# The second expert choice of a two-layer mixture counts per expert on the partitions, and the constants of the choices are copied by ScalarE

## The chip, the cores and the metric

One core of a Trainium2 chip runs the whole program. The metric is the device time of one execution in microseconds (us); the engines are PE (TensorE matmul, with PEld for its weight loads), DVE (VectorE), ACT (ScalarE), POOL (GpSimd) and SP (SyncE, which issues DMAs).

## The reference, cut to what matters

Attention runs over 4 x 768 tokens of 8 heads, then a first mixture of experts, then a second one. The change lies in the second mixture. Each expert of it takes at most 384 of the 3072 tokens, and the (token, expert) pairs are served in the order of their logits:

```
cap = N // E                      # 384 tokens per expert, 8 experts
order = np.argsort(-logits.flatten())
for idx in order:
    tok, e = idx // E, idx % E
    if assigned[tok] >= 0 or counts[e] >= cap: continue
    assigned[tok] = e; counts[e] += 1
for e in range(E):
    mask = assigned == e
    out[mask] = np.maximum(x[mask] @ w1[e], 0.0) @ w2[e]
```

## The kernel before, in words

The attention and the first mixture fill the first 324 us of the profile and are not touched. The second mixture is `phase_d`, with the choosing in the class `Route2`.

**The choosing.** The greedy order is followed in eight phases. A phase finds the expert that fills up first, which tokens it gets, and takes both out of the logits `Lm` (128 partitions x 8 experts x 24 columns of tokens). To find where the first expert fills up, a phase searches a threshold on each token's best logit `v`: `NSTEP` = 5 steps, each with 32 candidate thresholds `thr` (L788). `g` (L793) marks for each of 24 token columns which thresholds each token reaches; `oh` (L783) marks each token's best expert. Matmuls of `g` with `oh` over the 128 partitions count, for each threshold, how many tokens each expert would get.

- Phase 0 counts with 24 matmuls a step (L802) that put thresholds on the partitions and experts on the columns, marks the thresholds with a full expert (L812), and one more matmul with ones (L825) counts those and spreads the number to all partitions. L826 turns it into the new lower bound `lo`.
- Phase 1, as `wide(1)` is 2, takes two token columns at once: 12 matmuls a step (L806), a subtraction (L809), a maximum over the experts (L815), a comparison (L823), and then the same matmul with ones (L825) and L826. PE is thus visited twice in a step, DVE works between the two visits, and both visits stand in PE's in-order queue.
- Phases 2 to 6 take four columns at once and count the full thresholds on DVE, with a 32x32 transpose (L820) and a reduction (L821) in place of the matmul with ones.

After the steps come `hi`, the marks of the tokens above the bounds (L831, L833), sums over them (L836, L842), the chosen expert `ei` (L849), and each token's place (L855 to L864). `ei` starts the load of that expert's weights from SP; `list` (L875) turns the places into row numbers, by which POOL gathers the token rows `xg` (L939).

**The experts.** An expert is `L1` (32 quarters: eight 128-column pieces of the hidden layer, four quarters each, a quarter being the three matmuls L961, L962, L963 of 384 columns) and `L2` (24 thirds of three matmuls of 512 columns, L975 to L977). Weights are split in high and low parts by ACT (`wh`, L923) and POOL (`wl`, L932). After each fourth quarter ACT writes `dhh` (L966) and DVE `dhl` (L968).

**The order of the work.** One loop at the end of `phase_d` writes the program, with a clock of its own, `now`. A quarter adds 0.5 to it. The choosing is a generator: each `yield lat,dur` gives the DVE time `lat` until its next piece of PE work may follow, and the PE time `dur` of that piece. `step` adds `lat` to the DVE clock and sets the piece due 0.1 after that while expert 0 runs; once `now` has reached the due time, the loop writes the piece into the program and adds `dur` to `now`. Each `dhl` adds 0.5 to the DVE clock. So these two numbers set how many quarters stand between two pieces of the choosing. All engines then run their queues in order.

Phase 1 is written while expert 0 runs, and its tail and `list(1)` come in expert 0's `L2`. The four constants `c8`, `jr`, `colid` and `p0` are copied into the PSUM tile `st_ps` by DVE at the start of phase 0 (L752, L754), behind the exit of the loop of L709, which ran no round here.

Of the kernel before, what the change touches and what calls it, by code (L numbers as in the profile page):

```python
# [6 lines left out]
F32=mybir.dt.float32; BF=mybir.dt.bfloat16; F32R=mybir.dt.float32r; I32=mybir.dt.int32; U32=mybir.dt.uint32  # L7
# [38 lines left out]
def phase_a(nc,tc,ctx,I,st):  # L46
    V=nc.vector; A=nc.scalar; T=nc.tensor; G=nc.gpsimd
    cl=ExitStack(); ld=cl.enter_context(tc.tile_pool(name="a_ld",bufs=2,side="right"))
# [7 lines left out]

    wm=K2[1][:,0].rearrange("p a b->p (a b)")[:,0:256]; V.memset(wm,1.0); wm=wm.bitcast(BF)
    def spin(k,wm=wm):
        p=ps.tile([128,4,128],F32,name="s_ps").rearrange("p a b->p (a b)")
        for _ in range(k): T.matmul(p,wm[:,0:128] if len(wm.shape)==2 else wm[:,0,0:128],wm,start=True,stop=True)  # L60
    spin(WARM)
    for i in range(2):
        t=cp.tile([128,2,12,128],F32,name=f"Q2_{i}"); Q2.append(t)
        for h in range(2):
            (G if i else V).memset(t[0:64,h,:,64:128],0.0); G.memset(t[64:128,h,:,0:64],0.0)
    for i in range(3):
# [7 lines left out]
    def load(u):  # L74
# [3 lines left out]
        def ld_k(h0,h1): nc.sync.dma_start(kt[:,h0:h1],I['k'][b,:,2*g+h0:2*g+h1,:])  # L78
# [10 lines left out]
        if u==0: nc.sync.dma_start(cst,I['cst'])  # L89
        if u==2: yield; prep_v(1,V)  # L90
        ld_k(1,2); ld_q(1,2)
# [7 lines left out]
    def prep_k(u,h):  # L99
        d=U[u]; kt,ks=d['kt'],d['ks']  # L100
        V.tensor_reduce(ks[:,h],kt[:,h,39:39+S].rearrange("p (n k)->p n k",k=32),AX.X,OP.max)
    def prep_k2(u,h,cpy):
# [10 lines left out]
    def prep_v(u,eng):  # L113
        d=U[u]; vn,vv=d['vn'],d['vv']
        vs2=wk.tile([96,64],F32,name="vs2",bufs=2); w=1024
        if eng is V: V.tensor_reduce(vs2,vn[:,w:2*w].rearrange("p (k d)->p d k",d=64),AX.X,OP.add); w//=2
        while w>=64:
            G.tensor_tensor(vn[:,0:w],vn[:,0:w],vn[:,w:2*w],op=OP.add); w//=2  # L118
        if eng is V: G.tensor_tensor(vn[:,0:64],vn[:,0:64],vs2,op=OP.add)
        G.tensor_scalar(vs2,vn[:,0:64],1.0/32,None,op0=OP.mult)  # L120
        for h in range(4):
            nc.sync.dma_start(vv[0:24,:,h,0:64],vs2[24*h:24*h+24,None,:].to_broadcast([24,12,64]))
# [612 lines left out]
class Route2:  # L735
    def __init__(self,nc,tc,cp,wk,ps,I,st):
        self.nc,self.tc,self.cp,self.wk,self.ps,self.st=nc,tc,cp,wk,ps,st
        cc=st['cc']
        self.jr=cc[:,0:32]; self.wsc=cc[:,32:37]; self.p0=cc[:,37:38]
        self.Lm=st['Lm']; self.asg=st['asg']; self.r=st['rrow']  # L740
        self.pos={}
        st['io']=cp.tile([128,8,3],I32,name="io"); self.th=cp.tile([128,2],F32,name="th")
        self.ws=cp.tile([128,5],F32,name="ws"); self.nM=cp.tile([128,1],F32,name="nM")

        q=ps.tile([128,512],F32,name="st_ps",bufs=1); o=0; self.q={}
        for nm,w in (('v',24),('jr',32),('c8',8),('mx',24),('gl',48),('tm',24),('sat',8),('s8',8),('dm',48),('fo',8),('kp',24),('x0',24),('an',24),('pos',24),('si',24),('bi',24),('sf',24),('bf',24),('colid',24),('p0',1),('oc',12)):
            self.q[nm]=q[:,o:o+w]; o+=w
    def state(self,nm,dt=None):
        return self.q[nm].bitcast(dt) if dt else self.q[nm]
    def init_state(self):  # L750
        V=self.nc.vector; st=self.st
        for nm,src in (('c8',st['c8']),('jr',self.jr)): V.tensor_copy(self.q[nm],src)  # L752
        yield
        for nm,src in (('colid',st['colid']),('p0',self.p0)): V.tensor_copy(self.q[nm],src)  # L754
        yield
    def wide(self,ph): return 2 if ph<3 else 4
    def psum(self):
        return self.ps.tile([128,512],F32,name="rt_ps",bufs=1)
# [9 lines left out]
    def phase(self,ph):  # L768

        nc,st,wk=self.nc,self.st,self.wk; V=nc.vector; T=nc.tensor  # L770
        B3=[128,8,24]; B4=[128,2,8,24]; Lm=self.Lm; c8=st['c8']
        ini=self.init() if ph==0 else iter(()); inq=self.init_state() if ph==0 else iter(()); Q=self.state
        next(inq,None)
        v=Q('v'); V.tensor_reduce(v,Lm.rearrange("p e c->p c e"),AX.X,OP.max)
        if ph: yield 0.4,0
        cand=wk.tile(B3,BF,name="p_cand"); V.tensor_tensor(cand,Lm,v[:,None,:].to_broadcast(B3),op=OP.is_ge)
# [4 lines left out]
        mx=Q('mx'); V.tensor_reduce(mx,cand.rearrange("p e c->p c e"),AX.X,OP.max)  # L781
        next(ini,None)
        oh=wk.tile(B3,BF,name="p_oh"); V.tensor_tensor(oh,cand,mx[:,None,:].to_broadcast(B3),op=OP.is_equal)  # L783
        th=self.th; lo=th[:,0:1]; hi=th[:,1:2]; ws=self.ws
        if ph<7:
            low=self.nM
            for s in range(NSTEP):
                thr=wk.tile([128,32],F32,name="p_thr"); V.tensor_scalar(thr,Q('jr'),ws[:,s:s+1],low,op0=OP.mult,op1=OP.add)  # L788
                if s==0: yield 1.3,0
                g=wk.tile([128,24,32],BF,name="p_g")  # L790
                for c0,c1 in (((0,12),(12,20),(20,24)) if ph==0 else ((0,24),)):
                    B=[128,c1-c0,32]
                    V.tensor_tensor(g[:,c0:c1],v[:,c0:c1,None].to_broadcast(B),thr[:,None,:].to_broadcast(B),op=OP.is_ge)  # L793
                if s==0: next(inq,None)
                nw=self.wide(ph) if ph>=1 else 1
                yield ((2.3+0.2*nw if ph>=2 else 1.4) if s else 1.1),(0.7 if ph<1 else 0.8/self.wide(ph))
                p=self.psum()

                anys=wk.tile([J,1],BF,name="p_any")
                if ph<1:  # L800
                    if ph==0: T.matmul(p[0:J,0:8],st['mone'][:,0:J],st['capr'],start=True,stop=False)
                    for c in range(24): T.matmul(p[0:J+(ph>0),0:8],g[:,c,0:J+(ph>0)],oh[:,:,c],start=(ph>0 and c==0),stop=(c==23))  # L802
                else:

                    n=self.wide(ph)
                    for c in range(0,24,n): T.matmul(p[0:32*n,0:8*n],g[:,c:c+n,:].rearrange("p c j->p (c j)"),oh[:,:,c:c+n].rearrange("p e c->p c e"),start=(c==0),stop=(c==24-n))  # L806
                    d=wk.tile([128,8],F32,name="p_d"); x=self.r
                    for q in range(n-1,0,-1):
                        V.tensor_tensor(d[32*q-32:32*q],x[32*q:32*q+32],p[32*q:32*q+32,8*q:8*q+8],op=OP.subtract); x=d  # L809
                if ph==0:  # L810
                    sat=wk.tile([J,8],BF,name="p_sat")
                    V.tensor_scalar(sat,p[0:J,0:8],0.0,0.0,op0=OP.is_ge,op1=OP.max,accum_out=anys)  # L812
                else:
                    R=32; sat=wk.tile([32,8],F32,name="p_sat1"); e=wk.tile([32,1],F32,name="p_e")
                    V.tensor_tensor_reduce(out=sat,in0=p[0:R,0:8],in1=self.r[0:R] if ph<1 else d[0:R],scale=1.0,scalar=-1e9,op0=OP.subtract,op1=OP.max,accum_out=e)  # L815
                if ph>=2:

                    an=wk.tile([128,1],F32,name="p_an4")
                    for q in range(4): V.tensor_scalar(an[32*q:32*q+R],e,0.0,None,op0=OP.is_ge)
                    tr=wk.tile([128,32],F32,name="p_tr"); V.transpose(tr,an.to_broadcast([128,32]))  # L820
                    p=wk.tile([128,1],F32,name="p_cnt"); V.tensor_reduce(p,tr[:,0:J],AX.X,OP.add)  # L821
                else:
                    if ph: V.tensor_scalar(anys,e[0:J],0.0,None,op0=OP.is_ge)  # L823
                    yield (0.7 if ph else 0.35),0.05
                    p=self.psum(); T.matmul(p[:,0:1],st['ones_b'][0:J,:],anys,start=True,stop=True)  # L825
                V.tensor_scalar(lo,p[:,0:1],ws[:,s:s+1],low,op0=OP.mult,op1=OP.add); low=lo  # L826
            V.tensor_scalar(hi,lo,ws[:,NSTEP-1:NSTEP],None,op0=OP.add)
        else:
            for x in (lo,hi): V.tensor_copy(x,self.nM)
        gl=Q('gl').rearrange("p (s c)->p s c",s=2); gs=wk.tile([128,2,24],F32,name="p_gl")  # L830
        for x in (gl,gs): V.tensor_tensor(x,v[:,None,:].to_broadcast([128,2,24]),th[:,:,None].to_broadcast([128,2,24]),op=OP.is_ge)  # L831
        og=wk.tile(B4,BF,name="p_og"); rs=wk.tile([128,2,8],BF,name="p_rs")
        V.tensor_tensor(og,oh[:,None,:,:].to_broadcast(B4),gl[:,:,None,:].to_broadcast(B4),op=OP.mult)  # L833
        if ph: yield (3.0 if 2<=ph<7 else 1.0),0
        with nc.allow_low_precision("counts up to 24 are exact"):
            V.tensor_reduce(rs,og,AX.X,OP.add)  # L836

# [4 lines left out]
        p=self.psum(); T.matmul(p[:,0:16],st['ones_b'],rs.rearrange("p s e->p (s e)"),start=True,stop=True)  # L842
# [3 lines left out]
        dm=Q('dm').rearrange("p (s c)->p s c",s=2); t2=wk.tile([128,2],BF,name="p_t2")  # L846
# [4 lines left out]
        fo=Q('fo'); V.tensor_scalar(fo,s8,m8,None,op0=OP.is_equal)  # L851
# [7 lines left out]
        kp=Q('kp'); V.scalar_tensor_tensor(kp,x[:,1],float(CAP),dm[:,1],op0=OP.is_le,op1=OP.mult)  # L859
        x0=Q('x0'); V.tensor_mul(x0,x[:,0],dm[:,0])  # L860
        V.tensor_mul(x[:,1],x[:,1],kp)
        pos=Q('pos',I32)
# [265 lines left out]
```

## Time and profile before

| | |
|---|---|
| median of 3 runs | 687.71 us (686.41 to 689.97) |
| the profiled execution, its own time | 682.42 us |
| its span, first to last instruction | 680.8 us |
| granted TensorE clock, mean over the span | 0.946 |
| PE, DVE, ACT, POOL busy | 604.4, 508.0, 314.2, 359.0 us |

The time of an execution is the span and 1.6 us around it. A group of instructions in a row of the profile is named by its line, engine and operation, then out<-in by the program's tile names. Matmuls overlap: one of 384 columns lasts 0.34 us in the rows and the next starts 0.17 us after it.

### The profile page before, as it was taken

What the parts mean: (1) busy time and instruction counts of PE and PEld (TensorE: products, weight loads), DVE (VectorE), ACT (ScalarE), POOL (GpSimd) and SP (SyncE); (2) the same over time, 40 slices, a digit from 0 to 9 for tenths busy, and PEclk for the clock granted to TensorE, in tenths of its full rate; (3) what the DMA queues carried; (4) which work ended last, traced back from release to release, by engine and by line L of the source; (5) the groups of instructions that cost most, each with busy time, mean ns of one, the idle gap of its engine ahead of it and who ended that gap; (6) DMA issues with size and microseconds to landing.
All of it is one profiled execution on the core that took longest, in us unless ns stands there. A gap on an engine that the chain in (4) does not pass through costs nothing.

```text
span 680.8 us, 12765 instructions
## 1 busy us (share of the span) xinstructions
PE 604.4 (89%) x4424; PEld 494.0 (73%) x4427; DVE 508.0 (75%) x1896; ACT 314.2 (46%) x672; POOL 359.0 (53%) x388
## 2 busy tenths in 40 slices
PE   8769896899788999989447999999999999999996
PEld 5658775778466776666226778888797978879895
DVE  5788985999896899994675778788888888862120
ACT  6557774787235676461014235162533426154521
POOL 5234323535462463761016359494876939399841
PEclk9889997999689999898559999999999999999999
DMA  9999999969309968610026063453626254385201
GB/s 258 256 241 249 241 234 206 281 115 339 136 16 324 294 207 287 204 62 23 2 87 208 2 227 115 166 175 124 202 76 203 79 187 155 139 258 180 105 1 46
DMA packets 59778, 114.22 MB, mean 168 GB/s; under 512 B 13537, under 2 KB 23521, under 8 KB 58944
## 3 DMA queue, kind: packets, MB, share of 16 engines
q1 hardware_dynamic: 49968, 79.37, 40.6%
q0 software_dynamic: 9744, 34.02, 15.1%
q8 instruction: 35, 0.57, 0.4%
q14 instruction: 31, 0.25, 0.1%
HBM read 96.54 MB, written 14.88 MB: 164 GB/s over the span
## 4 chain that ended last, share of the span: by engine, by line
PE 18%; issue 11%; POOL 11%; DVE 6%; DMA 3%; ACT 1%; POOLq 1%; DVEq 0%
POOL wl L932 9%; PE dh_ps L961 3%; PE dh_ps L962 3%; PE dh_ps L963 3%; DMA xg<-xrows,p_ix 2%; PE dz_ps L975 2%; PE dz_ps L976 2%; PE dz_ps L977 2%; POOL out_dram L982 2%; DMA wraw<-in_w1b_dram 1%; DVE p_g L793 1%; PE rt_ps L806 1%; PE dx_ps L895 1%; PE dh_ps L950 1%; ACT wh L923 1%
## 5 line engine op out<-in xcount | busy, mean ns | idle before, releaser
L932 POOL TENSOR_TENSOR wl<-wraw,wh 128x512 fp32r<-128x512 f32 x124 | 155.4, 1297 | 5.9 <-ACT wh L923 5.5
L961 PE MATMUL dh_ps<-dxh,wh 128*128 128x384 f32 x256 | 89.2, 349 | 0.7 <-ACT dxh L953 0.7
L923 ACT CAST wh<-wraw 128x512 fp32r<-128x512 f32 x128 | 73.7, 620 | 33.8 <-DMA wraw<-in_w1b_dram 33.4
L962 PE MATMUL dh_ps<-dxl,wh 128*128 128x384 f32 x256 | 86.3, 337 | 0.5 <-DVE dxl L953 0.5
L963 PE MATMUL dh_ps<-dxh,wl 128*128 128x384 f32 x256 | 86.1, 336 | 0.0
L118 POOL TENSOR_TENSOR wraw<-wraw 96x512 f32<-96x512 f32 (+4 forms) x39 | 39.9, 1023 | 80.2 <-DMA wraw<-in_v_dram 77.8
L975 PE MATMUL dz_ps<-wh,dhh 128*128 128x512 f32 x192 | 79.0, 411 | 0.0
L977 PE MATMUL dz_ps<-wh,dhl 128*128 128x512 f32 x192 | 76.0, 396 | 0.0
L976 PE MATMUL dz_ps<-wl,dhh 128*128 128x512 f32 x192 | 75.9, 395 | 0.0
L968 DVE SCALAR_TENSOR_TENSOR dhl<-dh_ps,dhh 128x384 fp32r<-128x384 f32 x64 | 35.1, 554 | 49.0 <-ACT dhh L966 48.7
L982 POOL DMA_INDIRECT out_dram<-dz,io x24 | 24.5, 1023 | 79.5 <-ACT dz L980 76.8
L966 ACT ACTIVATE dhh<-dh_ps 128x384 fp32r<-128x384 f32 x64 | 31.5, 492 | 75.7 <-PE dh_ps L963 74.8
L505 POOL TENSOR_TENSOR wl<-wraw,wh 128x512 fp32r<-128x512 f32 (+1 forms) x26 | 47.8, 1861 | 26.2 <-ACT wh L504 22.7
L980 ACT COPY dz<-dz_ps 128x512 f32<-128x512 f32 x24 | 14.1, 587 | 102.8 <-PE dz_ps L977 56.8
L138 ACT ACTIVATE p_e<-s_sb,nm 128x118 f32<-128x118 f32 x192 | 59.7, 385 | 1.1 <-DVE nm L132 1.1
L128 PE MATMUL s_ps<-kt,Q 128*128 128x118 f32 x192 | 41.4, 299 | 11.6 <-DVE kt L108 9.1
L939 POOL DMA_INDIRECT xg<-xrows,p_ix x24 | 23.3, 972 | 50.9 <-DVE rrow L871 31.3
L961 PEld LDWEIGHTS dh_ps<-dxh,wh 128*128 128x128 f32 x256 | 48.4, 189 | 1.5 <-ACT dxh L953 0.9
L962 PEld LDWEIGHTS dh_ps<-dxl,wh 128*128 128x128 f32 x256 | 48.2, 188 | 1.3 <-DVE dxl L953 1.1
L963 PEld LDWEIGHTS dh_ps<-dxh,wl 128*128 128x128 f32 x256 | 48.1, 188 | 0.0
L504 ACT CAST wh<-wraw 128x1024 fp32r<-128x1024 f32 (+1 forms) x48 | 44.2, 983 | 7.3 <-DMA wraw<-in_w1a_dram 7.1
L132 DVE CUSTOM_DVE_ANT_0 s_sb<-s_ps,cst 128x118 f32<-128x118 f32 x192 | 42.0, 275 | 5.3 <-PE s_ps L128 3.5
(359 smaller groups left out, 1466.5 us busy)
## 6 DMA issues: line engine op xcount, KB each, us to landing
wraw<-in_w1b_dram SPq DMA_DIRECT2D x15, 1024.0 KB
wraw<-in_w2b_dram POOLq DMA_DIRECT2D x14, 1024.0 KB, 7.5
wraw<-in_w2a_dram SPq DMA_DIRECT2D x12, 1024.0 KB
wraw<-in_w1a_dram SPq DMA_DIRECT2D x10, 1024.0 KB
VV<-in_v_dram SPq DMA_DIRECT2D x16, 585.0 KB
kt<-in_k_dram SPq DMA_DIRECT2D x16, 412.0 KB
qd<-in_q_dram SPq DMA_DIRECT2D x16, 384.0 KB
wraw<-in_v_dram SPq DMA_DIRECT2D x8, 768.0 KB
```

What stands on the lines that cost most here:

```text
L132: V.tensor_tensor_reduce(out=sb[:,j,:],in0=p[:,j,0:118],in1=mk,scale=-0.125,scalar=3e38,op0=OP.add,op1=OP.min,accum_out=nm[:,j:j+1])
L138: A.activation(pe[:,j,:],sb[:,j,:],AF.Exp,bias=nm[:,j:j+1],scale=-1.0)
L504: (hi.tensor_copy if hi else nc.scalar.copy)(h[:,c],t[:,c])
L505: (lo or nc.vector).tensor_tensor(l[:,c],t[:,c],h[:,c].bitcast(F32),op=OP.subtract)
L923: A.copy(h[:,c],t[:,c])
L932: eng.tensor_tensor(l[:,c],t[:,c],h[:,c].bitcast(F32),op=OP.subtract)
L961: T.matmul(q,wh[:,c],s['xh'][:,d,:],start=(d==0),stop=False)
L962: T.matmul(q,wh[:,c],s['xl'][:,d,:],start=False,stop=False)
L963: T.matmul(q,wl[:,c],s['xh'][:,d,:],start=False,stop=(d==3))
L975: T.matmul(q,s['hh'][:,f,c0],wh[:,c],start=(f==0),stop=False)
L976: T.matmul(q,s['hh'][:,f,c0],wl[:,c],start=False,stop=False)
L977: T.matmul(q,s['hl'][:,f,c0],wh[:,c],start=False,stop=(f==7))
```

## The change

In phase 1 the experts stand on the partitions in place of the thresholds. `oh` is copied four times by ACT into `oh4`, 24 columns of 4 x 8 weights. Each step has 96 matmuls: for each of the 24 token columns, four with 32 weight columns and 32 moving columns, each of the four writing its own 32 partitions of `p`, so that every partition holds the counts of expert (partition mod 8) for 32 thresholds. `rc`, made once, holds that expert's remaining room on the same partition. One DVE operation compares and counts (`cn`), a transpose and a maximum over 32 spread the largest count, and `lo` follows. L809, L815, L823 and the matmul with ones L825 are gone from phase 1, and each step visits PE once. The planner's numbers for phase 1 change: 1.9 and 1.1 for a step (1.4 and 0.4, then 0.7 and 0.05 before) and 1.6 before the sums (1.0 before).

The four constants go to PSUM by four ACT copies at the start of phase 0, in place of two DVE copies there and two after `g` of phase 0's first step.

```
+... ('p0',1),('oc',12),('sat1',32)):
     def init_state(self):
-        V=self.nc.vector; st=self.st
-        for nm,src in (('c8',st['c8']),('jr',self.jr)): V.tensor_copy(self.q[nm],src)
-        yield
-        for nm,src in (('colid',st['colid']),('p0',self.p0)): V.tensor_copy(self.q[nm],src)
-        yield
+        A=self.nc.scalar; st=self.st
+        for nm,src in (('c8',st['c8']),('jr',self.jr),('colid',st['colid']),('p0',self.p0)): A.copy(self.q[nm],src)
...
+        if ph==1:
+            rc=wk.tile([128,32],F32,name="p_rc"); V.transpose(rc,self.r[:,None,:].to_broadcast([128,4,8])); rc=rc[:,0:1]
+            oh4=wk.tile([128,24,4,8],BF,name="p_oh4")
+            for q in range(4): nc.scalar.copy(oh4[:,:,q],oh.rearrange("p e c->p c e"))
...
-                yield ((2.3+0.2*nw if ph>=2 else 1.4) if s else 1.1),(0.7 if ph<1 else 0.8/self.wide(ph))
+                yield ((2.3+0.2*nw if ph>=2 else 1.9 if ph else 1.4) if s else 1.1),(0.7 if ph<1 else 1.1 if ph<2 else 0.8/self.wide(ph))
                 p=self.psum()
+                if ph==1:
+                    for c in range(24):
+                        for q in range(4): T.matmul(p[32*q:32*q+32,0:32],oh4[:,c].rearrange("p r e -> p (r e)"),g[:,c,:],start=(c==0),stop=(c==23))
+                    cn=wk.tile([128,1],F32,name="p_cn"); sx=Q('sat1')
+                    V.tensor_scalar(sx[:,0:J],p[:,0:J],rc,0.0,op0=OP.is_ge,op1=OP.add,accum_out=cn)
+                    tr=wk.tile([128,32],F32,name="p_tr"); V.transpose(tr,cn.to_broadcast([128,32]))
+                    p=wk.tile([128,1],F32,name="p_cnt"); V.tensor_reduce(p,tr,AX.X,OP.max)
+                    V.tensor_scalar(lo,p,ws[:,s:s+1],low,op0=OP.mult,op1=OP.add); low=lo
+                    continue
...
-        if ph: yield (3.0 if 2<=ph<7 else 1.0),0
+        if ph: yield (3.0 if 2<=ph<7 else 1.6),0
```

## Rows read from the trace of the kernel before

**Rows 1.** Windows: length, each engine's busy us (instructions), granted clock, DMA share, GB/s.
```profile
368.75:408.89 40.14, 39.53 (x263) 32.05 (x263) 29.96 (x111) 12.56 (x24) 21.01 (x22) 1.00 0.31 103
...
410.90:660.00 249.10, 247.29 (x1398) 215.73 (x1399) 176.73 (x682) 102.21 (x197) 183.37 (x182) 1.00 0.43 145
```

**Rows 2.** Timeline of PE in phase 1: start, us, instructions [idle before, releaser].
```profile
364.90 0.57 PE L806 MATMUL rt_ps<-p_oh,p_g 128*64 128x16 bf16 x12
...
368.75 0.17 PE L825 MATMUL rt_ps<-p_any,ones_b 31*128 31x1 bf16 x1 [2.05 <-DVE p_any L823]
...
370.18 0.34 PE L962 MATMUL dh_ps<-dxl,wh 128*128 128x384 f32 x1
370.35 0.34 PE L963 MATMUL dh_ps<-dxh,wl 128*128 128x384 f32 x1
370.64 0.57 PE L806 MATMUL rt_ps<-p_oh,p_g 128*64 128x16 bf16 x12
371.13 0.44 PE L961 MATMUL dh_ps<-dxh,wh 128*128 128x384 f32 x1
...
386.43 0.39 PE L975 MATMUL dz_ps<-wh,dhh 128*128 128x512 f32 x1
```

**Rows 3.** Timeline of ACT and DVE before the first step's second visit to PE.
```profile
364.98 2.18 ACT L923 CAST wh<-wraw 128x512 fp32r<-128x512 f32 x4 [3.49 <-DMA wraw<-in_w1b_dram]
...
367.58 0.56 DVE L968 SCALAR_TENSOR_TENSOR dhl<-dh_ps,dhh 128x384 fp32r<-128x384 f32 x1 [4.50 <-ACT dhh L966]
368.17 0.15 DVE L809 TENSOR_TENSOR p_d<-rrow,rt_ps 32x8 f32<-32x8 f32 x1
```

**Rows 4.** Single lines (min/median/max ns, first and last start) and the DVE timeline of phase 2.
```profile
L847 DVE TENSOR_SCALAR_CACHE_REDUCE st_ps<-asg,p_m x16: 245/245/248, 345.0 to 597.4; 128x24 f32<-128x24 bf16 x16
L847 DVE DVE_READ_ACCUMULATOR st_ps<-asg,p_m x16: 142/143/146, 345.1 to 597.6; 128x1 bf16 x16
...
402.62 0.21 DVE L820 STREAM_TRANSPOSE p_tr<-p_an 128x32 f32<-128x32 f32 x1
...
403.74 0.96 DVE L793 TENSOR_TENSOR p_g<-st_ps,p_thr 128x768 bf16<-128x768 f32 x1
```

**Rows 5.** Timelines of PE and one line of ACT: small operations.
```profile
310.39 0.43 PE L611 MATMUL yt_ps<-yT,wg 128*32 128x128 f32 x8
330.35 0.82 PE L802 MATMUL rt_ps<-p_oh,p_g 128*31 128x8 bf16 x24 [1.49 <-DVE p_g L793]
405.41 0.66 PE L950 MATMUL dh_ps<-cb,xg 128*128 128x128 f32 x4
...
L193 ACT ACTIVATE g_d<-g_d 128x48 f32<-128x48 f32 x3 | 0.7, 243 | 11.5 <-DVE g_d L192 11.5
```

**Rows 6.** The start of phase 0: the loop's exit on PE and ACT, then DVE's timeline.
```profile
L709 PEldq COMPARE_BRANCH  x2: 187/248/310, 325.6 to 327.3; - x2
...
L709 ACTq COMPARE_BRANCH  x1: 38/38/38, 325.6 to 325.6; - x1
...
326.18 0.17 DVE L752 COPY st_ps<-cb 128x8 f32<-128x8 f32 x1
...
326.61 0.62 DVE L774 TENSOR_REDUCE st_ps<-Lm 128x24 f32<-128x192 f32 x1
...
328.36 0.29 DVE L763 TENSOR_REDUCE i_a<-rt_ps 128x1 f32<-128x128 f32 x1 [0.34 <-PE rt_ps L762]
...
331.20 0.15 DVE L812 TENSOR_SCALAR_CACHE_REDUCE p_sat<-rt_ps 31x8 bf16<-31x8 f32 x1
```

**Rows 7.** Timeline of PE at the border from expert 0 to expert 1.
```profile
409.52 0.56 PE L806 MATMUL rt_ps<-p_oh,p_g 128*64 128x16 bf16 x12 [0.46 <-DVE p_g L793]
...
410.72 0.44 PE L962 MATMUL dh_ps<-dxl,wh 128*128 128x384 f32 x1 [0.26 <-DVE dxl L953]
```

**Rows 8.** Windows around an idle PE in the first mixture, columns as in rows 1.
```profile
191.12:193.77 2.65, 0.01 (x2) 0.01 (x1) 2.65 (x16) 0.60 (x1) 0.63 (x2) 1.00 0.01 3
193.79:197.20 3.41, 3.41 (x35) 3.20 (x36) 2.01 (x10) 1.37 (x3) 0.96 (x1) 0.50 0.09 19
```

More of the change, by code (lines that the diff above doesn't have):

```diff
@@ L745, in __init__ @@
         q=ps.tile([128,512],F32,name="st_ps",bufs=1); o=0; self.q={}
-        for nm,w in (('v',24),('jr',32),('c8',8),('mx',24),('gl',48),('tm',24),('sat',8),('s8',8),('dm',48),('fo',8),('kp',24),('x0',24),('an',24),('pos',24),('si',24),('bi',24),('sf',24),('bf',24),('colid',24),('p0',1),('oc',12)):
+        for nm,w in (('v',24),('jr',32),('c8',8),('mx',24),('gl',48),('tm',24),('sat',8),('s8',8),('dm',48),('fo',8),('kp',24),('x0',24),('an',24),('pos',24),('si',24),('bi',24),('sf',24),('bf',24),('colid',24),('p0',1),('oc',12),('sat1',32)):
             self.q[nm]=q[:,o:o+w]; o+=w
@@ L771, in phase @@
         B3=[128,8,24]; B4=[128,2,8,24]; Lm=self.Lm; c8=st['c8']
-        ini=self.init() if ph==0 else iter(()); inq=self.init_state() if ph==0 else iter(()); Q=self.state
-        next(inq,None)
+        ini=self.init() if ph==0 else iter(()); Q=self.state
+        if ph==0: self.init_state()
         v=Q('v'); V.tensor_reduce(v,Lm.rearrange("p e c->p c e"),AX.X,OP.max)
@@ L793, in phase @@
                     V.tensor_tensor(g[:,c0:c1],v[:,c0:c1,None].to_broadcast(B),thr[:,None,:].to_broadcast(B),op=OP.is_ge)
-                if s==0: next(inq,None)
                 nw=self.wide(ph) if ph>=1 else 1
-                yield ((2.3+0.2*nw if ph>=2 else 1.4) if s else 1.1),(0.7 if ph<1 else 0.8/self.wide(ph))
+                yield ((2.3+0.2*nw if ph>=2 else 1.9 if ph else 1.4) if s else 1.1),(0.7 if ph<1 else 1.1 if ph<2 else 0.8/self.wide(ph))
                 p=self.psum()
+                if ph==1:
[7 more added lines that the diff above has]
+                    continue
                 anys=wk.tile([J,1],BF,name="p_any")
```

## The prediction

> **What bounds the kernel now.** I read the windows by stage first. From 368.75 us, in the middle of expert 0's first layer, PE is busy for 39.53 of 40.14 us, and from 410.90 to 660 for 247.29 of 249.10, at full granted clock [rows 1]. So what counts is how much PE time the second choice takes out of expert 0: every wait that it makes on PE goes to the end of the kernel one for one, and work taken off DVE or ACT counts only where PE waits for it.
>
> The timeline of PE in phase 1 comes next. A quarter of the first layer is three matmuls whose starts lie 0.17 apart, 0.52 us. A step's first visit (L806) takes PE from 370.35 + 0.17 = 370.52 to 371.13, 0.61 us; its second (L825) some 0.2, its own 0.17 and the step to the next. In the first step PE also stands still for 2.05 us before L825 [rows 2]. The timelines of DVE and ACT say why: the landing of weights let ACT start four casts at 364.98, the first `dhh` stood behind them, DVE did `dhl` at 367.58 and only then, in its order, L809 at 368.17 [rows 3].
>
> **The change, step by step: PE's visits.** Gone are five visits L825, 5 x 0.2, and the first one's wait. Each L806 becomes 96 matmuls. The trace has none of 32 by 32 in this form. The nearest are eight with 32 weight columns and 128 moving ones, each writing one quarter of the partitions: 0.43 us for all eight, while four of 128 moving columns on the whole array take 0.66 [rows 5]. That is 0.054 each against 0.165, with the run of the last one counted in both, so the quarters of the array do work side by side. A pair of load and matmul that has no other beside it takes (0.57 - 0.17)/11 = 0.036 in L806 and (0.82 - 0.17)/23 = 0.028 in L802 [rows 2, 5]. I take 24 fours of 0.03, 0.72, and the two ends of a visit, 0.61 - 11 x 0.036 = 0.21: 0.93 us a step. Bounds: 0.88, and 2.9 to 3.7 if all 96 pairs stand one after another. The work on PE grows from 5 x 0.81 = 4.05 to 4.65.
>
> Here a rule speaks against the change. The eight matmuls of L611 overlap though all of them use all 128 rows [rows 5]. The Trainium skill, page "TensorE: Matmul & The Clock Gate", section "Part 3: Packing small matmuls — row/col tiling", says that a weight load overlaps matmuls in flight only when the row group differs; by it the 96 pairs would follow one another, the upper bound, where the row gives 0.93. The row does not bear the rule out, so I go by the row; what the other would mean is a rival below.
>
> **DVE between two visits.** After the counts a step needs the comparison with its sum (like L847, 0.25, and 0.14 to read the sum), then transpose, maximum, `lo`, `thr` and `g`, which in phase 2 run from 402.62 to 404.70 [rows 4]: 0.39 + 2.08 = 2.47 us. In the first step the comparison stands where L809 stood, behind the same `dhl`, at 368.17, and `g` is done at 370.64. That is just when the second L806 starts in the kernel before [rows 2]. So the wait of 2.05 us is not gone: it moves to the next visit.
>
> How much PE does meanwhile is set by the planner. After a visit `now` has grown by 1.1, and the next is due 1.9 + 0.1 later: four quarters of 0.5 (a `dhl`'s 0.5 falls inside these and doesn't count). The visits will stand after quarters 5, 9, 13, 17 and 21. Before, by the same arithmetic with 0.4, 0.7, 0.05 and 1.4, they stood after 5, 10, 16, 21 and 26.
>
> So: first visit at 364.90; PE has it and four quarters behind it at 364.90 + 0.81 + 2.06 = 367.8, and waits until 370.65, 2.85 us, some 2.7 of them idle, as the last matmul still runs. From there a visit repeats after 0.70 + 0.17 (the last count's end) + 0.04 + 2.47 + 0.05 = 3.44 us, while PE has 0.93 + 2.06 = 3.0 of work: it waits some 0.45 in each of three. The fifth visit is at 370.65 + 3 x 3.44 = 381.0. With 0.81 and the 11 quarters left (5.7) the first layer ends at 387.5, and the visit L842 (0.2), which then stands inside it, makes that 387.7. Before, it ends at 386.43 with L842 still ahead, 386.6 [rows 2]. **The choice costs +1.0.** Bounds: -0.5, if five quarters stand between visits and nothing waits, and +2.1, if `dhl` waits for ACT's casts and adds 0.3 to each cycle.
>
> `oh4` and `rc`: four ACT copies, each near the 0.24 of L193 [rows 5], and 0.21 of DVE like L820 [rows 4]. Both engines then wait for the gathered rows of expert 0, so 0; without that cover they cost 1 us.
>
> **The start.** Two DVE copies before L774 go, 326.61 - 326.18 = 0.43 us. But DVE already waits 0.34 for PE's L762 before it starts L763 at 328.36, and PE is held by its own exit from the loop until 327.5 at the earliest (327.3 + 0.19) [rows 6]. DVE would only wait longer: 0, not -0.43. The other two copies end as the first counts do (L802 ends at 330.35 + 0.82 = 331.17, L812 starts at 331.20): 0 [rows 5, 6]. ACT leaves the loop at 325.6 and needs some 4 x 0.24. If all accesses to `st_ps` are kept in order, L774 starts at about 326.7 in place of 326.61, and the 0.34 hides that too. Bounds: -0.4, if L762 follows DVE after all, and +0.5, if the copies end only at 327.5.
>
> **The border.** The planner's clock gives phase 1 more PE time than before, 5 x (1.1 - 0.4 - 0.05) = 3.25, so its tail, the load and the gather for expert 1 are written five thirds of the second layer (0.65 each) earlier. PE is busy there; this buys only the waits at the border, 0.46 and 0.26 [rows 7]. I take -0.5, since `dxl` comes sooner; bounds 0 and -0.7.
>
> Sum: +1.0 + 0 - 0.5 = +0.5 on the profiled execution's 682.42 (its span of 680.8 and 1.6 around it): 682.9. The median of the runs shown, 687.71, lies 5.3 above that execution; I carry the difference over: **688.2 us**.
>
> **The rivals.**
> - *The clock falls.* PE's new idle time is longer than the old. After 2.65 us without work in the first mixture the clock stood at 0.50 for 3.41 us [rows 8]; after the 2.05 before L825 it did not fall [rows 1, 2]. 3.41 us at half speed lose 1.7, of which a wait of 0.45 hides part: +1.3, 689.5.
> - *The wait really goes (the other side).* If enough quarters stand between the first and the second visit, or the first `dhh` is not behind the casts, PE loses neither the 2.05 nor its successor: -2.05 + 0.6 for the visits, -0.7 at the border: -2.1, 685.6. For it speaks that the visit which waited is gone; against it the planner's four quarters, and the landing at 364.98 that the change doesn't move. It decides from 2.85 / 0.52 = 5.5 more quarters.
> - *The 96 matmuls run one after another.* A visit of 2.9 to 3.7 makes a cycle of 5.4 to 6.1, in which four quarters hardly wait. The fifth visit comes at 386.9 to 389.0, and expert 0 ends 9 to 12 later: 696 to 699. For it speaks only that L611's moving part is four times as long and its burst short. This is what the Trainium skill's rule named above would do here.
> - *The ACT copies are late*, behind ACT's exit from the loop: +0.5, 688.7.
>
> **How the numbers follow.** Forecast 0.50, the clock falls 0.22, the wait goes 0.13, one after another 0.08, late copies 0.07. A measurement of this kernel can tell about 0.5% (3.4 us) from no change. The forecast's own bounds reach from -1.6 to +2.6, 686.1 to 690.3. The range takes in the case in which the wait goes and the one in which the clock falls with its bounds (+1.3 and some +2), and the spread of the runs (1.3 below and 2.3 above their median), and leaves out the case of matmuls one after another: 684.9 to 692.0. Below 684.3 lies the lower half of the case in which the wait goes, and 0.03 of the others: 0.10. Above 691.1 lie the 96 in a row, 0.08, and a third of the clock's case: 0.15. The rest, 0.75, can't be told from no change.
>
> **What would show it.** On PE: a step's 96 matmuls in 0.9 us, a wait of 2 to 3 us before the second step's, visits after quarters 5, 9, 13, 17 and 21, and from the first quarter of expert 0 to its second layer 0.8 to 1.5 us more than before. At the start: L763 as far behind the loop's exit as before. I am wrong if the second visit finds `g` ready, if a step's matmuls last over 1.5 us, if the clock drops near 371, or if the waits at the border grow.

## The result and the profile after

The changed kernel takes 695.46 us (median of 5 runs, 693.21 to 698.48) beside 687.95 (686.41 to 689.97) of the kernel before: a ratio of 1.0113, with a 95% interval of 1.0074 to 1.0151. The change is slower by some 7.5 us. The prediction, 688.2 with a range of 684.9 to 692.0, is wrong: its likeliest case was no change that can be told, and its range ends below the result.

| | before, as shown | after |
|---|---|---|
| the profiled execution, its own time | 682.42 us | 697.96 us |
| its span | 680.8 us | 696.3 us |
| granted TensorE clock, mean over the span | 0.946 | 0.931 |
| PE, DVE, ACT, POOL busy | 604.4, 508.0, 314.2, 359.0 us | 613.1, 506.3, 317.5, 361.4 us |

The two profiled executions lie 15.5 us apart, twice what the runs say. Part of that is the spread of single executions ahead of the change: `Lm`, the last addition to the logits with which the second mixture's choosing starts, is reached at 325.8 us before and at 332.6 after, in code that nobody touched, and between 324.9 and 332.6 in the thirteen profiles of this study, the old code among the late ones too (329.9 in experiment 6). The lower mean clock is no mark of the change either: the old code of experiment 6 was granted 0.931 too. So all that follows is counted from `Lm` on, in stages, for every profile. The windows of the kernel after, from `Lm` to expert 0, then expert 0, 1, 2 and 3, 4, 5 and 6, 7, and last from expert 1's first matmul to PE's last one:

```profile
core 0: us, PE busy (x) PEld busy (x) DVE busy (x) ACT busy (x) POOL busy (x), PEclk, DMA share, GB/s
332.55:370.07 37.52, 15.16 (x185) 10.19 (x185) 27.49 (x102) 6.11 (x15) 5.55 (x7) 0.59 0.28 87
370.07:419.83 49.76, 47.63 (x723) 40.42 (x724) 36.85 (x131) 16.15 (x31) 27.97 (x27) 0.95 0.43 145
419.83:460.12 40.29, 39.88 (x250) 34.75 (x249) 32.30 (x127) 16.28 (x31) 28.34 (x29) 1.00 0.45 148
460.12:541.67 81.55, 77.62 (x439) 66.25 (x438) 65.70 (x263) 31.93 (x61) 54.84 (x57) 1.00 0.41 136
541.67:581.09 39.42, 38.65 (x221) 33.26 (x219) 32.30 (x127) 15.11 (x29) 27.70 (x29) 1.00 0.44 144
581.09:657.24 76.15, 74.05 (x391) 64.45 (x390) 40.30 (x151) 32.50 (x62) 59.93 (x60) 1.00 0.49 162
657.24:690.83 33.59, 33.59 (x169) 29.98 (x167) 4.46 (x8) 9.22 (x18) 14.81 (x17) 1.00 0.06 24
419.83:690.83 271.00, 263.79 (x1465) 228.69 (x1463) 175.06 (x673) 105.05 (x201) 185.63 (x187) 1.00 0.40 132
```

The same windows of the kernel before, in the profile of its second copy (experiment 1), for experts 2 and 3, 5 and 6, and the whole from expert 1 on; last, the whole in the profile shown first:

```profile
453.44:531.32 77.88, 77.17 (x440) 66.39 (x439) 66.67 (x267) 31.20 (x60) 55.37 (x56) 1.00 0.45 148
...
570.32:644.64 74.32, 73.67 (x391) 64.08 (x390) 40.05 (x150) 32.43 (x62) 58.17 (x58) 1.00 0.48 164
...
411.20:678.25 267.05, 264.79 (x1467) 229.85 (x1464) 177.67 (x685) 103.76 (x200) 186.31 (x187) 0.99 0.41 138
```
```profile
410.02:675.43 265.41, 263.34 (x1467) 228.17 (x1464) 177.55 (x685) 104.27 (x201) 186.38 (x187) 1.00 0.41 139
```

Before, PE was busy for nearly all of the time from expert 1 on [rows 1]. After, it is idle for 271.00 - 263.79 = 7.21 us there, where the kernel before has 265.41 - 263.34 = 2.07 in the profile shown and 2.26 in its second one. The loss lies in experts 2 and 3 and in 5 and 6, where the diff changes no instruction. What the change did to expert 0 comes near the forecast: 49.76 us from its first matmul to that of expert 1, 48.48 and 48.89 before.

The timeline of PE, the new visits of phase 1 (start, us, instructions, idle before and releaser):

```profile
375.47 0.93 PE L803 MATMUL rt_ps<-p_g,p_oh 128*32 128x32 bf16 x96
378.98 0.93 PE L803 MATMUL rt_ps<-p_g,p_oh 128*32 128x32 bf16 x96 [0.30 <-DVE p_g L795]
382.49 0.93 PE L803 MATMUL rt_ps<-p_g,p_oh 128*32 128x32 bf16 x96 [0.26 <-DVE p_g L795]
```

The 96 matmuls of a step take the 0.93 us that were forecast, a visit repeats after 3.51 (forecast 3.44), and PE waits some 0.3 at each of four visits, which with the end of the last matmul comes near the 0.45 of the forecast.

### The profile page after: what moved, and what is told of

Read it like the earlier page. It is cut to its first block, busy times and chain, and to the rows that moved or that the text cites. A ratio compares the mean times of both kernels' runs of the same rounds, so it can differ in the third digit from the quotient of the medians.

```text
span 696.3 us, 13616 instructions
## 1 busy us (share of the span) xinstructions
PE 613.1 (88%) x4842; PEld 503.7 (72%) x4842; DVE 506.3 (73%) x1893; ACT 317.5 (46%) x680; POOL 361.4 (52%) x390
## 4 chain that ended last, share of the span: by engine, by line
PE 16%; POOL 12%; issue 12%; DVE 6%; DMA 3%; ACT 1%; POOLq 1%; DVEq 0%; ACTq 0%
POOL wl L944 10%; DMA xg<-xrows,p_ix 3%; PE dz_ps L987 2%; PE dz_ps L988 2%; PE dz_ps L989 2%; PE dh_ps L973 2%; PE dh_ps L974 2%; PE dh_ps L975 2%; POOL out_dram L994 2%; DVE p_g L795 1%; PE dh_ps L962 1%; PE rt_ps L803 1%; PE rt_ps L818 1%; ACT wh L935 1%; PE rt_ps L814 1%
## 5 line engine op out<-in xcount | busy, mean ns | idle before, releaser
L128 PE MATMUL s_ps<-kt,Q 128*128 128x118 f32 x192 | 43.2, 310 | 4.9 <-DVE kt L108 4.1
```

What stands on the lines that cost most here:

```text
L128: T.matmul(p[:,j,0:118],d['q2'][:,h,w,:],d['k2'][:,h,w//2,:] if w%2 else d['kt'][:,h,64*w:64*w+118],start=True,stop=True)
```

## The experiments

All kernels are compared with the kernel before on their own chip; a run's ratio has its 95% interval behind it. Line numbers are those of each kernel: before, `list`'s second form is L898, the counts from phase 2 on L806, the transposes of gathered rows L950; in the changed kernel they are L910, L818 and L962. Phase 2 takes two columns at once like phase 1 (12 matmuls a visit); four at once begin with phase 3 (6 matmuls). "From expert 1 on" is always from its first matmul to PE's last one; the 265.4 and 271.0 of the expectations, which say "to the last instruction", are read so too. The code cuts are shortened.

The first four ran together. **1. The kernel before, once more**, without an edit.

> The kernel before, unchanged, for a second profile: which stages move by themselves. Every theory expects a ratio of 1.000. If the 6.8 us by which the profile after reached the second mixture later (332.6 against 325.8) is spread of runs, this profile moves there by several us too, and by less than 1 us from the first quarter of expert 1 to the end (265.4).

Measured: 1.0034 (0.9994 to 1.0073). So a ratio within some 0.4% of 1 says nothing here. Both expectations of the profile failed: it reaches `Lm` only 0.2 us later (experiment 6 shows the spread there), and from expert 1 on it takes 267.05 us, 1.6 more than the first. Expert 1 holds that (42.24 beside 40.67): TensorE's clock is granted at 0.50 there for 3.41 us from 412.90 on, and half of these, some 1.7 us, are lost against 1.00 by estimate.

**2. The changed kernel with later due times.**

```
-   yield ((2.3+0.2*nw if ph>=2 else 1.9 if ph else 1.4) if s else 1.1), ...
+   yield ((2.3+0.2*nw if ph>=2 else 2.4 if ph else 1.4) if s else 1.1), ...
...
-   if ph: yield (3.0 if 2<=ph<7 else 1.6),0
+   if ph: yield (3.0 if 2<=ph<7 else 2.1),0
```

> The changed kernel with its due times later, 2.4 in place of 1.9 a step and 2.1 in place of 1.6 before the sums: five quarters between two visits, so that the choosing of experts 2 to 7 stands in PE's order where it stood before (tail of phase 1 after quarter 33, list of expert 1 after the 46th piece). Theory of the order (the loss is that the choosing moved against the experts by five pieces): expert 0 costs 0 to 2 us more than before, from expert 1 to the end 265 to 267 us as before, ratio 1.000 to 1.005. Theory of the count (the 96 matmuls, the DVE chain and the four ACT copies themselves cost it): ratio 1.009 to 1.013 as in the change.

Measured: 1.0048 (1.0015 to 1.0082), and 267.63 us from expert 1 on, 0.6 more than the theory of the order names; experts 5 and 6 hold that (76.11), as the list of phase 7 does not go back to its old place. About half of the loss is gone with two numbers of the planner.

**3. The kernel before, with phase 2 put earlier.** Nothing of the count is changed.

```
-   if ph: yield (3.0 if 2<=ph<7 else 1.0),0
+   if ph: yield (3.0 if 3<=ph<7 else 1.0),0
```

> The kernel before with one number of the planner changed: phase 2's yield before the sums is 1.0 in place of 3.0. No counting is changed. From expert 2 on the choosing then stands in PE's order exactly where the changed kernel has it. Theory of the order: slower by 3.5 to 6 us, ratio 1.005 to 1.009, lost in experts 1 to 6. Theory of the count: ratio 1.000.

Measured: 1.0071 (1.0036 to 1.0106), and 271.17 us from expert 1 on. The old count in the new order is slow. That the sum equals the changed kernel's 271.00 is chance: the order is that of the changed kernel from the sums in expert 1 to expert 5, but not at phase 7, experts 5 and 6 lose nothing, and 2.9 us lie in expert 1 (43.59 beside 40.67), where the changed kernel loses none. Some 1.7 of these are again half clock (3.41 us at 0.50 from 442.26 on). What the two share is expert 3: PE waits 1.13 us for `p_g` there, 1.20 in the changed kernel, and not at all before.

**4. The changed kernel with the constants copied by DVE as before.** 

```
-   A=self.nc.scalar; for nm,src in (four constants): A.copy(self.q[nm],src)
+   V=self.nc.vector; for nm,src in (c8, jr): V.tensor_copy(self.q[nm],src); yield
+   for nm,src in (colid, p0): V.tensor_copy(self.q[nm],src); yield
```

> The changed kernel with the four constants copied by DVE as before: the new count alone. Theory of the order and theory of the count: as slow as the change, ratio 1.008 to 1.013. Theory of the copies (ACT's copies to PSUM delay the start): ratio 1.000 to 1.003.

Measured: 1.0109 (1.0061 to 1.0157), 270.53 us from expert 1 on. The ACT copies of the constants are no part of the loss.

Where these orders differ is read from PE's program order. The place of a piece of the choosing is the number of quarters and thirds of the expert that stand ahead of it (0 to 55), for experts 2 and 3; the last columns are what stands in expert 6 (xT are the transposes of gathered rows). Experiments 5, 9 and 11 have the places of before, 10 has those of the changed kernel with 0 and 34 in expert 6:

```
                      expert 2: count count sums place list xT | expert 3: count count list xT | expert 6: list xT
before                          6     13    25   29    41   49 |           6     13    41   49 |           0    34
changed, 4                      2     9     21   25    38   45 |           4     11    42   49 |           2    35
3, before with phase 2 early    2     9     21   25    38   45 |           4     11    42   49 |           0    34
2, later due times              6     13    25   29    41   49 |           6     13    41   49 |           2    35
7, further back              0, 9    17     28   32    43   51 |        0, 9    17    43   51 |           5    36
```

The second four ran together too. **5. The old order with the new count.** The 2.4 and 2.1 of experiment 2 stay for phase 1, and phase 7 gets its 1.0 back; from the sums of phase 1 on PE's order is then that of the kernel before, piece for piece.

```
-   if ph: yield (3.0 if 2<=ph<7 else 2.1),0
+   if ph: yield (3.0 if 2<=ph<7 else 2.1 if ph<2 else 1.0),0
```

> The changed kernel with the planner's numbers 2.4 for a step of phase 1, 2.1 before its sums and 1.0 before those of phase 7: from the sums of phase 1 on, the program order of PE is piece for piece that of the kernel before; only the five counts with 96 matmuls, their DVE work and the ACT copies are left of the change. Theory of the order (the loss comes from where the choosing stands among the pieces of experts 1 to 6): ratio to the kernel before 0.998 to 1.004, and from the first matmul of expert 1 to the last instruction 265 to 267.5 us, as in the two profiles of the kernel before (265.4, 267.1), with expert 6 no longer waiting for its gathered rows. Rival, the new count costs by itself: at least 1.005, with the loss before expert 1. Rival, any other cause in DVE or ACT behind expert 0: 269 us or more from expert 1 on.

Measured: 0.9983 (0.9955 to 1.0011), 267.21 us from expert 1 on. With the old order the whole loss is gone, the new count, its DVE work and all ACT copies in place. Against 2, which differs in one number of phase 7 and ran on another chip, that is 0.65% by the ratios, 4.5 us; the profiles show 1.4 of it in experts 5 and 6 (76.11 and 74.72), and 0.4 from expert 1 on as a whole.

**6. The kernel before with the constants copied by ACT**, and nothing else:

```
-   V=self.nc.vector; for nm,src in (c8, jr): V.tensor_copy(self.q[nm],src); yield
-   for nm,src in (colid, p0): V.tensor_copy(self.q[nm],src); yield
+   A=self.nc.scalar; for nm,src in (four constants): A.copy(self.q[nm],src)
```

> The kernel before with the four ACT copies of the constants in place of the four DVE copies, and nothing else. My prediction's 0 for the start: ratio 0.997 to 1.003, and from the first reduction of Lm to the start of L763's successor line 2.5 to 2.6 us as before (2.56). Rival, the copies come late behind ACT's exit from the loop: 0.5 us more there, which the ratio cannot show. Rival, the copies are a gain that the change's loss covers: under 0.997.

Measured: 1.0008 (0.9973 to 1.0042), and 2.58 us from `Lm` to the reduction that is L763 before (2.56 there): nothing, as forecast.

**7. The changed kernel with phase 2 and later put back by eight pieces.**

```
+   if ph==1: yield 3.2,0        # at the end of a phase
```

> The changed kernel with one more pause at the end of phase 1, so that the phases from 2 on stand some eight pieces later among the pieces of experts 1 to 5 than in the changed kernel, and three later than in the kernel before. If the loss is only that the choosing comes too early for the engines that feed it, this third place gives 1.000 to 1.005 and less waiting before the transposes of gathered rows. If any place but that of the kernel before loses, 1.007 or more, with waits at other lines.

Measured: 1.0139 (1.0091 to 1.0186). Later is no better than earlier. The transposes for expert 1 now stand behind the last pieces of expert 0 (55 and 56 of 56), PE waits 1.45 us for gathered rows between them and 0.82 for `dxh` behind them, and behind the first of these waits its clock is granted at 0.50, the lower of its two levels, for 10.24 us. That is one other place, with its own losses; that every other place loses, it doesn't show.

```profile
412.23:415.53 3.30, 2.48 (x11) 1.75 (x11) 2.29 (x5) 2.22 (x5) 2.79 (x4) 0.64 0.96 314
415.53:418.50 2.97, 2.93 (x12) 2.09 (x13) 0.67 (x1) 2.02 (x4) 2.94 (x4) 0.50 0.97 357
```

**8. The changed kernel, once more**, without an edit.

> The changed kernel once more, unaltered, beside the others on one chip. If its loss is its own: ratio 1.008 to 1.014, and 269.5 to 272 us from the first matmul of expert 1 to the last instruction (271.0 in its first profile) with the same waits before L962, L907 and L818. If the first profile was an unlucky execution, under 269.

Measured: 1.0091 (1.0056 to 1.0125), 273.01 us from expert 1 on, the expected range passed by 1 us, with the same waits: 1.76 us for gathered rows at 492.01 and 1.20 for `p_g` at 508.26 stand for the 0.99 at 493.51 and the 1.20 at 508.20 of the first profile. Behind the 1.76 the clock is granted at 0.50 for 3.41 us, some 1.7 us of the 273.01 that the first profile does not have.

The last three ran together. **9. The copies into `oh4` behind the casts of expert 0**, with the numbers of 5:

```
-   if ph==1: rc=...; oh4=...; for q in range(4): nc.scalar.copy(...)     # ahead of the steps
...
    if s==0: yield 1.3,0
+   if ph==1 and s==0: rc=...; oh4=...; for q in range(4): nc.scalar.copy(...)
```

> The kernel of the old order with the new count (planner's numbers 2.4, 2.1 and, for phase 7, 1.0), and rc and the four ACT copies into oh4 written one yield later, behind the casts and dxh of expert 0 instead of ahead of them. Theory: ahead of them the copies hold ACT from its four casts of expert 0's weights until oh is there, so wl and dxl come late: from the landing of the last gathered rows to the first matmul of expert 0 2.5 us instead of 1.85, and another 0.7 before the second one. Behind them 0.6 to 1.3 us go: landing to first matmul 1.9 us or less, the casts of expert 0 at 352 instead of 358, and a ratio to the kernel before of 0.995 to 1.000. Rival, that the rows' landing covers the copies, as I predicted: no difference to the kernel with the copies ahead. Rival, that the copies then delay the first count: the wait goes to the first 96 matmuls.

Measured: 1.0002 (0.9972 to 1.0032), beside 0.9993 for the copies ahead (11): the time does not tell them apart. The traces do, at the start of expert 0.

**10. The changed kernel with phase 7's number as before.**

```
-   if ph: yield (3.0 if 2<=ph<7 else 1.6),0
+   if ph: yield (3.0 if 2<=ph<7 else 1.6 if ph<2 else 1.0),0
```

> The changed kernel with the number 1.0 before the sums of phase 7, as before, and 1.6 only for phase 1. From phase 7 on PE's order is then that of the kernel before (list at 0 and transposes at 34 of expert 6), the rest is as changed. Theory: experts 5 and 6 together take 74.4 to 74.7 us instead of 76.1, POOL gathers for expert 7 ahead of its own lows, and the ratio falls by 0.002 to 0.004 from the changed kernel's 1.009 to 1.011. Rival, that phase 7's number does nothing: 76.1 us and the ratio of the changed kernel.

Measured: 1.0069 (1.0033 to 1.0106) where the changed kernel has 1.0113 and 1.0091. Experts 5 and 6 take 74.23 us in place of 76.15. One number that the planner uses in another phase too is 2 us of the loss; by the ratios alone, whose intervals overlap, it would not be told.

**11. The kernel of 5, once more**, without an edit.

> The kernel of the old order with the new count once more, for a second profile and beside the one with the copies behind the casts: ratio 0.996 to 1.003, 2.5 us from the landing of expert 0's rows to its first matmul, 266 to 268 us from the first matmul of expert 1 to the last instruction, and no wait before the second visit of phase 1.

Measured: 0.9993 (0.9961 to 1.0026), 267.23 us from expert 1 on. The count in the old order costs nothing and gives nothing that a ratio can tell, twice. The profiles from expert 1 on (267.21, 267.23 and, in 9, 267.39) lie 1.0 above the mean of the three of the old code (265.41, 267.05, 266.34).

The stages of all profiles, in us, from the starts of the matmuls named:

```
                     Lm to E0   E0    E1    E2+E3  E4     E5+E6  E7     E1 to PE's last
before               35.75    48.48  40.67  77.91  38.83  74.39  33.61  265.41
1  before again      36.29    48.89  42.24  77.88  39.00  74.32  33.61  267.05
6  ACT copies only   36.14    48.58  40.78  78.57  38.98  74.40  33.61  266.34
5  old order         36.73    47.90  40.64  79.14  39.12  74.72  33.59  267.21
11 the same again    36.68    48.45  40.81  79.22  38.84  74.77  33.59  267.23
9  copies behind     36.38    48.16  40.64  78.96  39.06  75.13  33.60  267.39
2  later due times   36.71    48.44  40.64  78.20  39.09  76.11  33.59  267.63
10 phase 7 as before 37.35    49.51  40.31  81.34  39.56  74.23  33.58  269.02
4  count only        36.69    49.47  40.14  81.19  39.52  76.09  33.59  270.53
after                37.52    49.76  40.29  81.55  39.42  76.15  33.59  271.00
8  after again       36.70    50.25  40.54  83.38  39.42  76.08  33.59  273.01
3  before, early 2   37.92    48.66  43.59  80.09  39.51  74.37  33.61  271.17
7  further back      36.66    52.09  44.36  79.88  39.50  77.13  33.59  274.46
```

## Why the prediction was wrong

**The step that failed** is the border: "its tail, the load and the gather for expert 1 are written five thirds of the second layer (0.65 each) earlier. PE is busy there; this buys only the waits at the border", costed at -0.5 with bounds 0 and -0.7. The five thirds were right, and the waits at the border did go. But what they move is not one border: the later phases stand at other places among the pieces of experts 1 to 4, and a number that phase 7 shares moves its list at the border of 5 and 6. From expert 1 on the kernel takes 271.00 and 273.01 us after, 265.41, 267.05 and 266.34 with the old code, 5.7 more by the means. Beside the same count in the old order (267.21, 267.23 and 267.39) 4.7 of these are the order's; the other 1.0 stays with the new code, and no ratio tells it from nothing. Experiment 3 shows from the other side that the order alone is slow (1.0071). The price lies mostly in waits of PE, as the groups of PE from expert 1 on say (busy, mean ns, idle before and releaser). Before, then after:

```profile
L806 PE MATMUL rt_ps<-p_oh,p_g 128*128 128x32 bf16 (+1 forms) x147 | 11.7, 226 | 0.2 <-DVE p_g L793 0.2
L950 PE MATMUL dh_ps<-cb,xg 128*128 128x128 f32 x72 | 11.1, 278 | 1.1 <-DMA xg<-xrows,p_ix 1.0
```

```profile
L818 PE MATMUL rt_ps<-p_oh,p_g 128*128 128x32 bf16 (+1 forms) x144 | 11.5, 227 | 1.3 <-DVE p_g L795 1.2
L962 PE MATMUL dh_ps<-cb,xg 128*128 128x128 f32 x72 | 11.4, 281 | 4.9 <-DMA xg<-xrows,p_ix 4.6
L910 PE MATMUL dx_ps<-l_bv,l_A 128*128 128x96 bf16 x30 | 5.9, 344 | 0.4 <-DVE l_bv L901 0.4
```

and the new count with the old order (11):

```profile
L818 PE MATMUL rt_ps<-p_oh,p_g 128*128 128x32 bf16 (+1 forms) x147 | 11.7, 227 | 0.4 <-DVE p_g L795 0.4
L962 PE MATMUL dh_ps<-cb,xg 128*128 128x128 f32 x72 | 10.9, 279 | 1.9 <-DMA xg<-xrows,p_ix 1.8
L910 PE MATMUL dx_ps<-l_bv,l_A 128*128 128x96 bf16 x30 | 5.9, 344 | 0.0
```

Five waits come with the new places every time: they stand in every profile that has the place and in none that has the old one, the first four with the old count too (3). They are those of the lists in experts 1 and 2 (0.32 and 0.35 us for `l_bv` after), of a count in expert 3 (1.20 for `p_g`), of the tokens' places in expert 4 (0.29 for `rrow`) and of the rows for expert 7 (1.36): together 3.5 us, beside the 4.7. Three places make most of the loss. The first is expert 3, where the counts moved from 6 and 13 to 4 and 11. Piece 4 ends the first 128 columns of the hidden layer, whose `dhh` stands on ACT behind four casts; `dhl` follows it on DVE, and the count's DVE work stands behind `dhl`. These are the rows of PE, ACT and DVE:

```profile
502.79 0.52 PE L818 MATMUL rt_ps<-p_oh,p_g 128*128 128x32 bf16 x6
...
508.20 0.52 PE L818 MATMUL rt_ps<-p_oh,p_g 128*128 128x32 bf16 x6 [1.20 <-DVE p_g L795]
...
501.43 2.19 ACT L935 CAST wh<-wraw 128x512 fp32r<-128x512 f32 x4
503.51 0.49 ACT L978 ACTIVATE dhh<-dh_ps 128x384 fp32r<-128x384 f32 x1
...
504.04 0.56 DVE L980 SCALAR_TENSOR_TENSOR dhl<-dh_ps,dhh 128x384 fp32r<-128x384 f32 x1 [1.77 <-ACT dhh L978]
504.63 0.17 DVE L821 TENSOR_TENSOR p_d<-rrow,rt_ps 32x8 f32<-32x8 f32 x1
...
507.18 0.96 DVE L795 TENSOR_TENSOR p_g<-st_ps,p_thr 128x768 bf16<-128x768 f32 x1
```

DVE idles 1.77 us in front of `dhl`, the counts that were ready at 503.3 are taken up at 504.63, and seven quarters later PE waits 1.20. In the old order (5) the same two visits stand at 493.36 and 497.48 and wait for nothing; `dhl` is done ahead of the counts, and DVE waits for PE:

```profile
493.03 0.56 DVE L980 SCALAR_TENSOR_TENSOR dhl<-dh_ps,dhh 128x384 fp32r<-128x384 f32 x1
493.91 0.17 DVE L821 TENSOR_TENSOR p_d<-rrow,rt_ps 32x8 f32<-32x8 f32 x1 [0.32 <-PE rt_ps L818]
```

It is the very mechanism that I had read in phase 1 [rows 3], met again in a phase that I had not looked at.

The second is the end of expert 2. The list moved from 41 to 38 and the first transposes from 49 to 45, a third (0.65 us) less between them. After, and in the old order (5):

```profile
482.67 1.17 PE L910 MATMUL dx_ps<-l_bv,l_A 128*128 128x96 bf16 x6 [0.35 <-DVE l_bv L901]
...
490.81 0.66 PE L962 MATMUL dh_ps<-cb,xg 128*128 128x128 f32 x4 [0.21 <-DMA xg<-xrows,p_ix]
...
493.51 0.66 PE L962 MATMUL dh_ps<-cb,xg 128*128 128x128 f32 x4 [0.99 <-DMA xg<-xrows,p_ix]
```
```profile
474.75 1.17 PE L910 MATMUL dx_ps<-l_bv,l_A 128*128 128x96 bf16 x6
...
482.83 0.66 PE L962 MATMUL dh_ps<-cb,xg 128*128 128x128 f32 x4 [0.73 <-DMA xg<-xrows,p_ix]
...
484.36 1.06 PE L962 MATMUL dh_ps<-cb,xg 128*128 128x128 f32 x8
```

From the start of the list to the end of the last transposes 11.50 us and 10.67. The list waits for DVE's `l_bv`, which it did not before, and the transposes for the last rows. How long these rows take differs from execution to execution, and so does this wait: 1.76 in the second profile after. That the order makes the rows late is not shown: experiment 3 has the same places in expert 2, and there PE waits 0.20 for rows and takes 10.32 us for this stretch, no more than the old code in the old order (10.26 to 10.38). With the new count it takes 10.63 to 11.29 in the old order and 11.22 to 12.17 in the new. Why PE waits longer for them with the new count stays open.

The third is the end, and there I misread the diff: I took 1.6 for phase 1's number, but the condition `2<=ph<7` leaves phase 7 to it as well. Phase 7's list moves from 0 to 2 of expert 6, and on POOL the gather for expert 7 falls behind expert 6's low parts. POOL after, then with phase 7's number as before (10):

```profile
623.68 13.83 POOL L944 TENSOR_TENSOR wl<-wraw,wh 128x512 fp32r<-128x512 f32 x11
637.67 1.00 POOL L951 DMA_INDIRECT xg<-xrows,p_ix  x1 [0.16 <-issue]
```
```profile
620.16 3.79 POOL L944 TENSOR_TENSOR wl<-wraw,wh 128x512 fp32r<-128x512 f32 x3
624.12 1.00 POOL L951 DMA_INDIRECT xg<-xrows,p_ix  x1 [0.16 <-issue]
```

PE waits 1.36 us for those rows at 641.21 after, and not at all in 10.

**The other steps.**
- *The choice, +1.0*: its parts were read rightly, its sum was too small, and the border hid it. Expert 0 as a whole takes 49.47 to 50.25 us in the four profiles that keep its order of after, 48.48 to 48.89 in the four of the old code: +1.1 by the means. But that is net of the waits at the end of expert 0, 0.69 to 1.54 us with the old code and none after, 1.15 by the means; the choice itself costs some 2.2, about its upper bound of +2.1. The visit's 0.93, DVE's way between two visits (2.43 us from 376.49 to the end of `p_g` at 378.92; forecast 2.47) and the waits were as forecast, at four visits in place of three. The first layer alone is some 3.0 longer (27.35 to 28.10 beside 24.23 to 25.19) where 0.8 to 1.5 was named. The tokens' places (L867) also fell into it, with a wait of 0.85 that the sum does not have, and the second layer got 1.9 shorter. The lower bound of the term, -0.5 with five quarters between visits, is near what 5 and 11 have as a whole: 47.90 and 48.45.
- *The wait of 2.05 us that moves to the second visit*: wrong, without effect on the sum. No wait of this size stood before a visit of phase 1 in any later profile, of either kernel. In the profile that I read PE had its full clock at the start of expert 0; in all twelve others the clock was granted at 0.50 for 3.41 or 6.83 us there and the quarters took longer, so that `dhl` came in time: in 1 it starts 6.17 us behind expert 0's first matmul, as in the profile read (6.04), but the first visit stands at 5.50 in place of 3.35. The old code's first layer takes 24.23 to 25.19 us that way (1, 3 and 6) and 24.89 with the wait: one is as dear as the other.
- *96 matmuls one after another*: did not happen, 96 pairs are done in 0.93 us, and that the measured 695.46 lies beside this rival's 696 to 699 is chance. The Trainium skill, page "TensorE: Matmul & The Clock Gate", section "Part 3: Packing small matmuls — row/col tiling", says that a weight load overlaps matmuls in flight only when the row group differs. The trace does not agree: a load takes 0.092 us in its rows and a matmul 0.18, all use all 128 rows, and 96 of each are done in 0.93.
- *The clock falls*: it does at expert 0, but with the old code too, so it isn't the change's. The rival stays at nothing there; later, it fell once behind a wait that came with the change (8, in expert 2).
- *The start and the constants on ACT*, 0: right. The reduction of `Lm` now waits for ACT's copies (1.22 us behind `Lm` in place of 0.82), and the reduction that is L763 before still starts 2.58 behind `Lm` (2.56 before), as the 0.34 of cover had it [rows 6].
- *`oh4` and `rc`*, 0: wrong in part. I named the gathered rows as their cover, but not what queues behind them on ACT: the four casts of expert 0's first weights. The copies take 1.76 us, where four of 0.24 were assumed. They wait for `oh`, and the casts, `wl` and `dxl` wait for the copies. Counted from `Lm` (324.89 in 11, 331.93 in 9) the casts start after 32.8 us in 11 and after 25.7 in 9, where the copies stand behind them. ACT in 11, then in 9:

```profile
356.01 1.76 ACT L786 COPY p_oh<-p_oh 128x192 bf16<-128x192 bf16 x4 [29.94 <-DVE p_oh L780]
357.68 2.17 ACT L935 CAST wh<-wraw 128x512 fp32r<-128x512 f32 x4
```
```profile
357.66 2.18 ACT L935 CAST wh<-wraw 128x512 fp32r<-128x512 f32 x4 [24.54 <-DMA wraw<-in_w1b_dram]
...
368.15 1.80 ACT L791 COPY p_oh<-p_oh 128x192 bf16<-128x192 bf16 x4
```

PE waits 1.48 and 0.45 us for `dxl` ahead of its first two matmuls of expert 0 in 11, and 0.67 for `dxh` alone in 9. That is up to 1.3 us, and nothing where the rows land late (after, PE waits 2.44 for the last rows and then 0.68 for `dxh`, as in 9); no ratio tells it.

**The sum.** From `Lm` to PE's last matmul the two profiles after take 359.1 us on average, the three of the old code 351.0: +8.1, of which 5.7 are from expert 1 on, 1.35 in expert 0, and 1.05 ahead of it, where the copies and the landing of the first gathered rows, which varies in every kernel, can't be parted. By the ratios it is 6 to 8 us. The new count with later due times and the old order (5, 9 and 11) takes 352.0: 7.1 of the 8.1 come with the planner's numbers, 4.7 of them from expert 1 on and 1.8 in expert 0.

**What stays open.** Why 2 and 5 are 4.5 us apart by their ratios and 0.4 by their profiles from expert 1 on: their intervals hardly miss each other, and 2 has one profile. Why the gathered rows for expert 3 make PE wait longer with the new code, even in the old order (0.68 to 1.15 us beside 0.32 to 0.45). And no version beats the kernel before: the best, 5 and 11, can't be told from it. The wait of 2.05 us, which the change could have spared, stands in one of the profiles only, and a new visit holds PE longer than the two old ones' work together (0.93 beside 0.61 and some 0.2); that this is the whole reason was not tried.

## What to carry to other kernels

In a program whose order is planned by a clock of guessed costs, an edit of a guess can move everything behind it; price it by writing down the new order to the end and looking at each place where a moved piece stands behind a wait of another queue, not at the next border alone. To tell the cost of new work from that of a new order, give the new work the old order (here three numbers), and the old work the new order (here one, for most of it); then compare stage by stage, as two sums can agree by chance. A wait read from one profile is a fact of one execution: before building a sum on it, see whether a second one has it.

## What was not expected of the hardware

A whole visit of 96 matmuls with 32 weight columns and 32 moving ones, each writing its own quarter of the partitions, takes 0.93 us, 0.75 without the run of the last one: one pair of load and matmul in 8 ns on average, though a single load lasts 92 ns in the rows. And the twelve later profiles, of old and new code alike, have PE at half clock (0.50 granted) for 3.41 or 6.83 us at the start of expert 0, behind its idle time for the gathered rows, where the one that was read first kept 1.00 throughout. What decides between the two was not tried.
